# RetNet into a mixture of experts on one core: first half of expert 0's w2 asked for before two stores, and its first block difference made before the last logits

## Chip, cores and metric

The kernel runs on one core of a Trainium2 chip. The metric is device time in microseconds (us), here the median of three runs of the kernel.

## Reference

The reference computes a RetNet recurrence over q, k, v of 4 batches, 8 heads, 768 tokens and head size 64, and feeds the 3072 rows of 512 features into a mixture of 8 experts, of which each row takes the one with the largest logit:

```
state = gamma * state + k[t]^T v[t]        # per batch and head
y[t]  = (q[t] @ state) / sqrt(64)
x = y as rows (3072, 512)
logits = x @ w_gate                        # (3072, 8)
e = argmax(logits),  gate = softmax(logits)[e]
out[row] = gate * (relu(x[row] @ w1[e]) @ w2[e])    # w1: 512x1024, w2: 1024x512
```

All inputs and the result are float32.

## The kernel before

The attention part runs in 12 steps (the loop over `s`, line 863). A step takes 128 tokens of two batches: masked scores, the state's part and the new state on TensorE (PE), masks on VectorE (DVE), copies out of PSUM on ScalarE (ACT), scaling of q and v on GpSimd (POOL). The rows x of a step are turned on DVE (`to_rows`, line 653) one step later, and `store` (line 659) writes them from SBUF to a DRAM tensor `x_d` by four transfers of 128 KB, issued by SyncE (SP). Later on POOL's indirect transfers (`gather`, line 175) fetch the rows of an expert from `x_d`. Logits are made for two steps at a time (`logits`, `logits_of`); `place` turns them into ranks and places of the rows per expert, in three rounds.

From line 825 on the order of the instructions on all five engines is that of the program text. Each engine works through its own list in order, and an instruction that waits holds up what stands behind it on its engine. SP's transfers share eight semaphores in turn, so each also waits for the landing of the eighth transfer before it.

Expert 0 has an early pass: its first 256 rows (`EARLY`), which the first two rounds have found, are computed while the last rows are still being placed. Its weights w1 are asked for in a quarter, a quarter and a half (lines 922 to 926), w2 in two halves of 1 MB (`weights2`, line 160, and `more_of_weights2`, line 165; the first half holds feature blocks 0 to 3). In the last step (`last`, s = 11) SP stores the rows of steps 9 and 10 and then asks for the first half of w2.

After the loop, lines 972 to 975 run `layer1` for eight feature blocks f. In the midst of each block's four matmuls `within_early(f)` (line 945) adds what belongs to the last rows: at f = 1 the transposes of the last logits, their sum over four parts on DVE (L685) with what `place` makes of it, the turn of the last rows, their store and the request for the second half of w2; at f = 3 to 5 ranks and counts, and at the end of f = 5 the list `src` of source rows and a gather of two tiles on POOL; at f = 7 the first operands of the second layer.

The second layer of these 256 rows, `pair` (line 382), is a 2x2 block product with seven block products instead of eight (Strassen-Winograd). It needs four sums of blocks of h (`halves_of_h`, line 290, written to `he`) and four differences of blocks of w2 (`halves_of_w`, line 300, written to `we`). Of these, `we[0]` = b12 - b11 needs the first half of w2 alone, `we[1]` = b22 - we[0] and `we[2]` = b22 - b12 need the second half too. `we[0..2]` and `he[0..2]` are made on DVE; `we[3]` = b21 - we[1] and then `he[3]` on POOL (lines 980, 981), behind four gathers (lines 962 and 979). `he[0]` and `he[1]` are made for three of the four blocks at f = 7 (line 967) and for the last one at line 976. In `pair` the PE products come in the order ya (from h and w2 as they are), yb (he[1], we[1]), yd (he[2], we[2]), yc, ya again, ye (we[3]), yf (he[3]). Between them DVE makes the gated sums `u` and the output parts (`part`, L396) and, as `spare`, 16 transposes of the expert's further rows into `xTa` (L237); with these and the last parts done, PE begins the first layer of the further rows of expert 0 (L265, at 147.9 us). Later experts are not touched by the change.

Of the kernel before, what the change touches and what calls it, by code (L numbers as in the profile page):

```python
# [53 lines left out]
def kernel(  # L54
# [105 lines left out]
    def weights2(pool, e, parts=1, now=None):  # L160
        w2t = pool.tile([P, 1, FT, DM], F32, tag="w2t", name="w2t")
        more_of_weights2(w2t, e, parts, range(parts) if now is None else now)
        return w2t

    def more_of_weights2(w2t, e, parts, now):
        for part in (ts(i, FT // parts) for i in now):
            nc.sync.dma_start(w2t[:, :, part, :], w2v[:, ds(e, 1), part, :])
# [4 lines left out]
    first = ctx.enter_context(tc.tile_pool(name="first", bufs=1))  # L172
# [127 lines left out]
    def halves_of_w(w2t, ws, which=range(4), by=nc.vector):  # L300

        ws = [w.rearrange("p (f d) -> p f d", f=FH) for w in ws]
        b11, b12, b21, b22 = (w2t[:, 0, ts(j, FH), ts(k, DH)] for j in range(2) for k in range(2))
        sums = (b12, b11), (b22, ws[0]), (b22, b12), (b21, ws[1])
        for i in which:
            by.tensor_tensor(out=ws[i], in0=sums[i][0], in1=sums[i][1], op=ALU.subtract)  # L306
        return ws
# [175 lines left out]
    with ExitStack() as actx:  # L483
# [33 lines left out]
        def scale_q(s, b, by=nc.gpsimd, parts=1):  # L517
            got = raw.pop(("q", s, b))
            qs = raw["qs", s, b] = att.tile([P, 2, H, D], F32, tag="qs", name="qs")
            for part in (ts(i, H // parts) for i in range(parts)):  # L520
                for e in range(2):
                    by.tensor_tensor(out=qs[:, e, part, :], in0=got[:, part, ts(e, D)], op=ALU.mult,  # L522
                                     in1=inner(dec[:, ts(2 * where[s][0] + e, H)][:, part], D))
# [8 lines left out]
        def ends(s):  # L532
            return 2 * where[s][0] + where[s][2] == NC - 1
# [11 lines left out]
        def fade():  # L545

            back = dec[:, ts(2 * NC - 1, H)].rearrange("p (a j) -> p j a", j=2)
            for j in range(2):
                fading.append(xT1[:, j, :].rearrange("p (a t) -> p a t", a=HP))
                nc.gpsimd.tensor_tensor(out=fading[j], in0=middle(causal[:, :], HP), in1=inner(back[:, j, :], P), op=ALU.mult)  # L550
# [18 lines left out]
        def turn_k(s, b):  # L569
            kT = att.tile([P, HP, P], F32, tag="kT", name="kT")  # L570
            tr = pairs_of("tr", 2, "trk")
            heads_first(raw["k", s, b], tr)
            nc.scalar.copy(out=kT, in_=tr)  # L573
            front[s, b] = kT
# [4 lines left out]
        def scores(s, b):  # L579
            kT, qT = front.pop((s, b)), q_of(s, b)  # L580
            sc = [pairs_of("sc", 4, "sc") for _ in range(2)]
            am = [att.tile([P, HP, P], F32, tag=f"am{j}", name=f"am{j}") for j in range(2)]
            for a in range(HP):
                for j, half in ((0, 0), (1, 1), (1, 0), (0, 1)):
                    r, keys = ts(j, D), ts(half, P // 2)
                    nc.tensor.matmul(sc[j][keys, a, :], lhsT=kT[r, a, keys], rhs=qT[r, a, :], start=True, stop=True)  # L586

            def mask():
                for j in range(2):
                    nc.vector.tensor_tensor(out=am[j], in0=sc[j], op=ALU.mult,  # L590
                                            in1=fading[j] if ends(s) else middle(causal[:, :], HP))

            return am, mask
# [3 lines left out]
        def outputs():  # L597
            return [ps("y", 2, "y").rearrange("p (b a t) -> p b a t", b=2, a=HB) for _ in range(2)]
# [60 lines left out]
        def store(s):  # L659
            m, b1, e = where[s]  # L660
            xg = x.pop(("g", s))
            for g in range(Q):
                nc.sync.dma_start(x_d[ts((2 * m + e) * 2 + b1, 2 * P), ts(g, P)].rearrange("(t l) r -> l t r", l=L),
                                  xg[ts(g, L), :, :, :].rearrange("p b q r -> p (b q) r"))
# [145 lines left out]
        def load_all(nm, s):  # L810
            for b in range(2):
                load(nm, s, b)
# [46 lines left out]
        def step(s, at):  # L859
            for _ in range(WHEN.get(s, "").count(at)):  # L860
                next(rest, None)

        for s in range(STEPS):
            last = s + 1 == STEPS
            if s + 2 < STEPS:
                if s % 2 and s + 3 < STEPS:
                    load_all("q", s + 3)
                load_all("v", s + 2)
                if s + 3 < STEPS:
                    load_all("k", s + 3)  # L870
            if s % 2 == 0 and s + 2 < STEPS:
                for b in range(2):
                    scale_q(s + 2, b)
            if s + 1 < STEPS:
                (as_it_is if ends(s + 1) else scale_both)(s + 1)
            if s in (1, 2):
                nc.gpsimd.memset(xs2[s % 2], 0.0)
            if s == 3:
                fade()
            if s:  # L880
                am = [scores(s, b) for b in range(2)]
                am[0][1]()
                am[1][1]()
                step(s, "n")
            if last:
                pad_ranks(acc[:, NR - 1, 0:2])
            y = outputs()
            steps = [s - 2, s - 1] if s and s % 2 == 0 else []
            if where[s][0] or where[s][2]:
                with_state(s, y)  # L890

            def ahead():
                for b in range(2):
                    turn_k(s + 1, b)

            def ahead_q():
                if s % 2:
                    for b in range(2):
                        turn_q(s + 1, b)

            if s:
                if steps:
                    logit = logits(steps)
                if last:
                    early_rows()
                else:
                    ahead()
                reduce = logits_of(*logit) if steps else lambda: None
                step(s, "p")
                if not last:  # L910
                    ahead_q()
                reduce()
                if s in NEXT:
                    rest = chain(rest, place(NEXT.index(s) - 1))
                step(s, "a")
                to_rows(s - 1)
                if 2 <= s <= PART:
                    store(s - 2)
                if s == PART:
                    store(s - 1)  # L920
                if s == PART + 1:
                    wa = [weights1(first, 0, 4, [0])]
                if s == PART + 2:
                    more_of_weights1(wa[0], 0, 4, [1])
                    store(s - 2)
                    more_of_weights1(wa[0], 0, 2, [1])
                if last:
                    store(s - 2)
                    store(s - 1)
                    wa.append(weights2(first, 0, 2, [0]))  # L930
            next_state(s)()
            step(s, "b")
            within(s, y, am, ahead if s == 0 else lambda: step(s, "w"))
            step(s, "c")
            if s == PART + 2:
                fetched()
# [4 lines left out]
        we = [att.tile([P, FH * DH], F32, tag=tag, name="we", bufs=bufs)  # L941
              for tag, bufs in [("q", 4)] * 4]


        def within_early(f):
            nonlocal ne, arm, src, far, which
            if f == 1:
                logits_of(*logit)()
                next(rest)
                to_rows(STEPS - 1)  # L950
                store(STEPS - 1)
                more_of_weights2(wa[1], 0, 2, [1])
            if f == 3:
                next(rest)
            if f == 4:
                ne = count()
                arm = arms(ne)
            if f == 5:
                next(rest)
                next(rest, None)  # L960
                src, far = sources(inv, "")
                gather(xs2[0], src, range(HALF, TC))
            if f == 6:
                which = regs(0)
            if f == 7:
                halves_of_w(wa[1], we, [0])
                halves_of_h(hTa, hs, [0, 1], blocks=slice(0, FH - 1))
                halves_of_w(wa[1], we, [1])

# [287 lines left out]
```

## Time and profile before

| | |
|---|---|
| runs | 447.82, 444.72, 446.83 us; median 446.83 us |
| the profiled execution | 447.64 us, of which the span of the trace is 445.9 us |
| busy PE / weight loads / DVE / ACT / POOL | 425.8 / 373.4 / 243.0 / 125.3 / 270.2 us |
| chain that ended last | PE 64% of the span |
| mean granted clock of PE | 0.985 |

Times in the rows are microseconds from the start of the span. Engines: PE matmuls, PEld the weight loads of PE, DVE, ACT, POOL, and SPq the issuing of transfers on SP. L306 is line 306 of the kernel.

### The profile page before, as it was taken

To read this page: it belongs to the slowest core of one execution; us is meant where nothing else is said; L and a number is where in the kernel's file an instruction comes from. 1 tells how busy PE (TensorE), PEld (TensorE's weight loads), DVE (VectorE), ACT (ScalarE), POOL (GpSimd) and SP (SyncE) were. 2 spreads that over 40 slices of the span, in tenths; PEclk is the share of its full clock that TensorE was granted. 3 is DMA by queue.
4 is the path that set the end of the run, shared out by engine and by line. 5 is a ranking of instruction groups with operands and counts; after the bars stand their busy time and mean duration, and the time that the engine had idled before them with its cause. 6 is when DMAs were issued, how large, how long until landed. Compare 5 with 4: busy or idle time off the path is not lost.

```text
span 445.9 us, 10584 instructions
## 1 busy us (share of the span) xinstructions
PE 425.8 (95%) x4027; PEld 373.4 (84%) x4027; DVE 243.0 (54%) x541; ACT 125.3 (28%) x284; POOL 270.2 (61%) x223
## 2 busy tenths in 40 slices
PE   7899898989999899999999999999999999999992
PEld 4789787878788868879998999997999999699681
DVE  4544879496689946713562464356256335533320
ACT  2456353454411212310321321034022114112310
POOL 4469526442037358594819883899996698579111
PEclk9999999899999899999999999999999999999997
DMA  9999999999953699366232972496395268120001
GB/s 198 235 232 204 232 219 212 247 222 282 271 163 93 209 398 359 99 230 193 111 81 60 309 254 65 106 374 189 103 355 172 50 170 335 32 91 0 5 30 51
DMA packets 113326, 80.72 MB, mean 181 GB/s; under 512 B 56874, under 2 KB 97834, under 8 KB 113200
## 3 DMA queue, kind: packets, MB, share of 16 engines
q1 hardware_dynamic: 104336, 65.31, 52.7%
q0 software_dynamic: 5520, 12.60, 8.4%
q10 hardware_dynamic: 3344, 1.36, 1.3%
q8 instruction: 52, 0.85, 0.8%
q14 instruction: 74, 0.61, 0.4%
HBM read 60.88 MB, written 15.99 MB: 172 GB/s over the span
## 4 chain that ended last, share of the span: by engine, by line
PE 64%; DVE 0%; ACT 0%; issue 0%; POOLq 0%
PE p L344 25%; PE p L390 19%; PE p L278 8%; PE p L265 7%; PE p L1021 6%; DVE xs L396 0%; POOLq L1253 0%; ACT o L283 0%; ACT o L284 0%; DVE u L396 0%; DVE gate L228 0%; DVE o L396 0%
## 5 line engine op out<-in xcount | busy, mean ns | idle before, releaser
L177 POOL DMA_INDIRECT xs<-x_d,src x30 | 32.0, 1067 | 19.7 <-issue 7.2
L348 DVE TENSOR_TENSOR hT<-p,q 128x196 f32<-128x196 f32 (+5 forms) x72 | 25.9, 360 | 31.4 <-PE p L344 31.2
L437 POOL DMA_INDIRECT out_dram<-o,dst x20 | 20.0, 998 | 34.9 <-ACT o L286 13.8
L522 POOL TENSOR_TENSOR qs<-q,dec 128x512 f32<-128x512 f32 x22 | 23.3, 1088 | 29.0 <-DMA q<-in_q_dram 18.0
L278 PE MATMUL p<-w2t,hT 128*24 128x128 f32 (+6 forms) x288 | 37.6, 357 | 0.0
L390 PE MATMUL p<-ws,hs 128*128 128x256 f32 x168 | 37.4, 379 | 0.0
L344 PE MATMUL p<-t,w1t 128*128 128x196 f32 (+5 forms) x192 | 35.8, 329 | 0.0
L344 PE MATMUL p<-t,s 128*128 128x196 f32 (+5 forms) x192 | 35.8, 329 | 0.0
L396 DVE SCALAR_TENSOR_TENSOR q<-p,gate,q 128x256 f32<-128x256 f32 x28 | 12.8, 479 | 41.8 <-PE p L390 26.3
L390 PEld LDWEIGHTS p<-ws,hs 128*128 128x128 f32 x168 | 31.9, 190 | 4.3
L590 DVE TENSOR_TENSOR am<-sc,causal 128x512 f32<-128x512 f32 x40 | 24.9, 683 | 16.1 <-PE sc L586 16.1
L306 POOL TENSOR_TENSOR ws<-w2t,ws 128x1024 f32<-128x1024 f32 x14 | 33.1, 2363 | 0.5
L306 POOL TENSOR_TENSOR ws<-w2t 128x1024 f32<-128x1024 f32 x14 | 33.2, 2369 | 0.1
L344 PEld LDWEIGHTS p<-t,s 128*128 128x128 f32 x192 | 32.4, 190 | 0.0
L344 PEld LDWEIGHTS p<-t,w1t 128*128 128x128 f32 x192 | 32.4, 190 | 0.0
L278 PEld LDWEIGHTS p<-w2t,hT 128*24 128x24 f32 (+6 forms) x288 | 18.6, 123 | 16.1 <-issue 14.7
L348 DVE TENSOR_TENSOR q<-p,q 128x196 f32<-128x196 f32 (+5 forms) x48 | 17.1, 358 | 24.2 <-PE p L344 15.7
L396 DVE SCALAR_TENSOR_TENSOR o<-p,gate,q 128x256 f32<-128x256 f32 x21 | 10.2, 484 | 34.4 <-PE p L390 29.6
L390 PE MATMUL p<-w2t,hT 128*128 128x256 f32 x112 | 26.9, 381 | 0.1
L586 PE MATMUL sc<-qT,kT 64*64 64x128 f32 x768 | 24.8, 273 | 1.6 <-ACT kT L573 1.4
L528 POOL TENSOR_TENSOR vs<-v,dec 128x512 f32<-128x512 f32 x19 | 19.7, 1045 | 10.2 <-DMA v<-in_v_dram 9.6
L1021 PE MATMUL p<-hT,w2t 128*128 128x136 f32 (+2 forms) x192 | 25.7, 295 | 0.0
(221 smaller groups left out, 899.1 us busy)
## 6 DMA issues: line engine op xcount, KB each, us to landing
w1t<-in_moe_w_dram SPq DMA_DIRECT2D x7, 2048.0 KB, 11.3
w2t<-in_moe_w_dram SPq DMA_DIRECT2D x7, 2048.0 KB
k<-in_k_dram SPq DMA_DIRECT2D x24, 256.0 KB, 4.6
v<-in_v_dram SPq DMA_DIRECT2D x24, 256.0 KB, 5.2
x_d<-xg SPq DMA_DIRECT2D x48, 128.0 KB, 3.0
q<-in_q_dram SPq DMA_DIRECT2D x11, 512.0 KB
xs<-xs SPq DMA_DIRECT2D x80, 64.0 KB, 2.1
w2t<-in_moe_w_dram SPq DMA_DIRECT2D x2, 1024.0 KB
```

The lines of the kernel that those rows point to most:

```text
L177: nc.gpsimd.indirect_dma_start(out=xs[:, t, :], out_offset=None, in_=x_d[0:rows, :], in_offset=bass.IndirectOffsetOnAxis(ap=idx[:, t : t + ...
L265: nc.tensor.matmul(hp, lhsT=w1t[:, 0, dt, ts(f, P)], rhs=xT[:, dt, n0:n], start=(dt == 0), stop=(dt == DT - 1))
L278: nc.tensor.matmul(y[j * z : j * z + m, 0:c], lhsT=hT[:, f, t * P + r0 : t * P + r0 + m], rhs=w2t[:, 0, f, ts(j, c)], start=(i == 0), stop ...
L306: by.tensor_tensor(out=ws[i], in0=sums[i][0], in1=sums[i][1], op=ALU.subtract)
L344: nc.tensor.matmul(rows(y), lhsT=a(d, f), rhs=b(d), start=start and d == 0, stop=d == 1, skip_group_check=True)
L348: nc.vector.tensor_tensor(out=to, in0=rows(y), in1=rows(plus), op=ALU.add)
L390: nc.tensor.matmul(y, lhsT=a[:, f, :], rhs=b[:, f, :], start=start and f == 0, stop=f == FH - 1, skip_group_check=True)
L396: nc.vector.scalar_tensor_tensor(out=to, in0=y, scalar=g[i], in1=plus, op0=ALU.mult, op1=ALU.add)
L522: by.tensor_tensor(out=qs[:, e, part, :], in0=got[:, part, ts(e, D)], op=ALU.mult, in1=inner(dec[:, ts(2 * where[s][0] + e, H)][:, part], D))
L586: nc.tensor.matmul(sc[j][keys, a, :], lhsT=kT[r, a, keys], rhs=qT[r, a, :], start=True, stop=True)
L590: nc.vector.tensor_tensor(out=am[j], in0=sc[j], op=ALU.mult, in1=fading[j] if ends(s) else middle(causal[:, :], HP))
L1021: nc.tensor.matmul(y, lhsT=w2t[:, 0, f, ts(dt, P)], rhs=hT[:, f, EARLY : EARLY + m], start=(i == 0), stop=(i == FT - 1))
```

## The change

In the last step the request for the first half of w2 is put ahead of the two stores on SP. On DVE the difference `we[0]` is taken from f = 7 to f = 0 of `within_early`, ahead of the sum of the last logits. Nothing else is touched.

```
                 if last:
+                    wa.append(weights2(first, 0, 2, [0]))
                     store(s - 2)
                     store(s - 1)
-                    wa.append(weights2(first, 0, 2, [0]))
...
         def within_early(f):
             nonlocal ne, arm, src, far, which
+            if f == 0:
+                halves_of_w(wa[1], we, [0])
             if f == 1:
                 logits_of(*logit)()
                 next(rest)
...
             if f == 7:
-                halves_of_w(wa[1], we, [0])
                 halves_of_h(hTa, hs, [0, 1], blocks=slice(0, FH - 1))
                 halves_of_w(wa[1], we, [1])
```

On SP, around the last steps of the attention part (`x_d<-xg` are the stores, four to a step; `128x4x512` is a half of w1 or of w2):

```order
 L663 DMA x_d<-xg 32x8x128 x4
 L158 DMA w1t<-in_moe_w_dram 128x4x512
-L663 DMA x_d<-xg 32x8x128 x8
 L167 DMA w2t<-in_moe_w_dram 128x4x512
-L663 DMA x_d<-xg 32x8x128 x4
+L663 DMA x_d<-xg 32x8x128 x12
 L167 DMA w2t<-in_moe_w_dram 128x4x512
 L158 DMA w1t<-in_moe_w_dram 128x4x1024
```

The first half of w2 stands right behind the second half of w1; the eight stores of steps 9 and 10 stand behind it, and the four of step 11 follow these directly.

On DVE, where the places of the early rows end (`dst_e`) and the sum of the last logits (L685) begins:

```order
 L206 SCALAR_TENSOR_TENSOR far_e<-ct_e,far_e 128x2
 L207 SCALAR_TENSOR_TENSOR dst_e<-bt_e,far_e 128x2
+L306 TENSOR_TENSOR we<-w2t 128x1024
 L685 TENSOR_REDUCE lg<-lg 128x32
 L702 TENSOR_REDUCE mx<-lg 128x8
```

The difference `we[0]` now stands ahead of the sum L685, and everything behind that sum stands behind it too.

On DVE, where the source rows of the last round are known (`src`) and the operands of the second layer begin (`he`):

```order
 L191 SCALAR_TENSOR_TENSOR src<-tok,far 128x32
 L192 TENSOR_TENSOR far<-inv,far 128x32
-L306 TENSOR_TENSOR we<-w2t 128x1024
 L297 TENSOR_TENSOR he<-hTa 128x384
 L297 TENSOR_TENSOR he<-he,hTa 128x384
```

Here `he[0]` follows the list of source rows directly; the lists of PE, ACT and POOL have the same order as before.

## Rows read from the trace of the kernel before

**Rows 1.** Busy time by windows: stretch; PE, PEld, DVE, ACT, POOL busy (instructions); clock; DMA

```profile
116.00:138.00 22.00, 22.00 (x133) 17.73 (x130) 16.56 (x59) 6.24 (x15) 7.05 (x10) 1.00 0.60 170
```

**Rows 2.** Timeline of SP's issues, 102 to 128 us: start, length, engine, line, tiles, count

```profile
107.70 0.63 SPq L158 DMA_DIRECT2D w1t<-in_moe_w_dram  x1
109.06 9.13 SPq L663 DMA_DIRECT2D x_d<-xg  x8
118.24 0.48 SPq L167 DMA_DIRECT2D w2t<-in_moe_w_dram  x1
```

**Rows 3.** DMA packets of two stretches, 111 to 114.5 us, then 120 to 124 us

```profile
DMA packets 1037, 1.34 MB, mean 382 GB/s; under 512 B 57, under 2 KB 538, under 8 KB 1036
...
DMA packets 508, 1.01 MB, mean 252 GB/s; under 512 B 16, under 2 KB 16, under 8 KB 508
```

**Rows 4.** Timeline, DVE around the last logits and a weight load of PE

```profile
117.33 0.16 DVE L207 SCALAR_TENSOR_TENSOR dst_e<-bt_e,far_e 128x2 uint32<-128x2 int32 x1
...
121.10 0.29 DVE L685 TENSOR_REDUCE lg<-lg 128x32 f32<-128x128 f32 x1 [3.60 <-PE lg L684]
...
128.22 1.23 PEld L781 LDWEIGHTS <-here 128*128 128x128 bf16 x8 [0.23 <-DVE here L762]
```

**Rows 5.** Timeline of POOL, 129 to 150 us

```profile
131.03 2.00 POOL L177 DMA_INDIRECT xs<-x_d,src  x1 [6.17 <-DVE far L192]
133.34 1.39 POOL L177 DMA_INDIRECT xs<-x_d,src  x1 [0.30 <-issue]
135.03 1.03 POOL L177 DMA_INDIRECT xs<-x_d,src  x1 [0.30 <-issue]
136.37 1.16 POOL L177 DMA_INDIRECT xs<-x_d,src  x1 [0.31 <-issue]
137.55 2.36 POOL L306 TENSOR_TENSOR we<-w2t,we 128x1024 f32<-128x1024 f32 x1
```

**Rows 6.** Timeline of DVE, 130.2 to 149 us

```profile
130.90 1.22 DVE L306 TENSOR_TENSOR we<-w2t 128x1024 f32<-128x1024 f32 x1
132.69 0.56 DVE L297 TENSOR_TENSOR he<-hTa 128x384 f32<-128x384 f32 x1 [0.57 <-ACT hTa L267]
133.28 0.56 DVE L297 TENSOR_TENSOR he<-he,hTa 128x384 f32<-128x384 f32 x1
...
135.43 1.22 DVE L306 TENSOR_TENSOR we<-w2t 128x1024 f32<-128x1024 f32 x1
136.56 0.68 DVE L297 TENSOR_TENSOR he<-hTa 128x512 f32<-128x512 f32 x1
137.54 0.88 DVE L396 SCALAR_TENSOR_TENSOR u<-yp,gate_e,m 128x256 f32<-128x256 f32 x2 [0.30 <-PE yp L390]
```

**Rows 7.** Timeline of PE and its weight loads: product yd and those behind it; further rows

```profile
137.30 3.32 PEld L390 LDWEIGHTS yp<-we,he 128*128 128x128 f32 x16 [0.28 <-DVE he L297]
...
147.93 9.00 PE L265 MATMUL p<-xTa,w1t 128*128 128x112 f32 x64 [1.73 <-DVE gate L228]
```

**Rows 8.** Timeline, 48.8 to 52.1 us: DVE beside POOL's products of q

```profile
48.84 0.22 DVE L703 TENSOR_TENSOR dl<-lg,mx 128x64 f32<-128x64 f32 x1
48.93 4.05 POOL L522 TENSOR_TENSOR qs<-q,dec 128x512 f32<-128x512 f32 x4 [4.66 <-PE new L623]
...
50.06 0.99 DVE L706 TENSOR_TENSOR top<-top,em 128x64 f32<-128x64 f32 x1
```

**Rows 9.** Timelines of DVE and of POOL, 303 to 307 us

```profile
304.22 0.69 DVE L297 TENSOR_TENSOR hs<-hT 128x512 f32<-128x512 f32 x1
304.82 1.10 DVE L297 TENSOR_TENSOR hs<-hT,hs 128x512 f32<-128x512 f32 x1
...
302.25 4.01 POOL L1036 TENSOR_SCALAR of<-ofr,gate 128x512 f32<-128x512 f32 x2
```

**Rows 10.** Busy time by windows, columns as in the first group, behind the pair

```profile
138.00:148.00 10.00, 8.27 (x39) 6.97 (x38) 9.64 (x25) 0.47 (x1) 5.18 (x4) 1.00 0.20 57
...
149.00:153.00 4.00, 4.00 (x24) 4.00 (x23) 3.93 (x6) 0.91 (x4) 3.64 (x7) 0.57 0.92 285
```

More of the change, by code (lines that the diff above doesn't have):

```diff
@@ L927 @@
                 if last:
+                    wa.append(weights2(first, 0, 2, [0]))
                     store(s - 2)
                     store(s - 1)
-                    wa.append(weights2(first, 0, 2, [0]))
             next_state(s)()
@@ L946, in within_early @@
             nonlocal ne, arm, src, far, which
+            if f == 0:
+                halves_of_w(wa[1], we, [0])
             if f == 1:
@@ L965, in within_early @@
             if f == 7:
-                halves_of_w(wa[1], we, [0])
                 halves_of_h(hTa, hs, [0, 1], blocks=slice(0, FH - 1))
```

## Prediction

> **What bounds the kernel now.** I read the windows first: from 116 to 138 us PE is busy in all of 22.00 us [rows 1], so in this stretch nothing ends sooner unless PE's own list gets shorter or a wait between its weight loads goes. From 138 to 148 us PE has 8.27 of 10 us and DVE 9.64 [rows 10]: there DVE is the bound, and the idle time of PE stands in one piece, the 1.73 us ahead of the first layer of the further rows, put down to DVE [rows 7]. So the path is PE until its product yb is there, which releases DVE's first `u` at 137.54 after 0.30 us of waiting, and from then on DVE: sums, sixteen transposes, parts, and at 147.93 PE again [rows 6, 7]. The reader should see that both moved pieces lie ahead of 137.54, where DVE isn't the bound as a whole but has two places without slack: the chain from the last logits to `here`, for which PE waits 0.23 us [rows 4], and `he[2]`, for which PE waits 0.28 us [rows 7].
>
> **The request on SP.** It moves from 118.24, behind eight stores, to right behind the second half of w1, whose issue ends at 107.70 + 0.63 = 108.33 [rows 2]. It has as many bytes as before. It is queued behind w1's half: between 111 and 114.5 us 1037 - 538 = 499 packets of 2 KB or more went through, about the 512 that such a half has, at 382 GB/s [rows 3]. From 114.5 on 1.05 MB take 2.75 us at that pace, and 4.2 us at the 252 GB/s of the stretch in which this transfer ran before [rows 3]: landed at 117.3 to 118.7. The stores of steps 9 and 10 go behind it; their rows are fetched by a gather at 131.03 [rows 5], so some 3 us of delay are covered by about 10. One store of step 10 has to wait for w2's landing, since it is the eighth transfer behind it; what is queued behind that store is the store of step 11, whose rows are turned on DVE only after the sum at 121.10. Cost 0. Without the queue's order, w2 would share the rate with the gather of the early rows; that is a rival below.
>
> **The difference ahead of the logits.** we[0] costs 1.22 us [rows 6]. DVE ends `dst_e` at 117.49 and then waits 3.60 us for PE's logits until 121.10 [rows 4]. With w2 landed at 117.3 to 118.7 it ends at 118.7 to 119.9, at least 1.2 us ahead of the sum. Cost 0, cover 1.2 us; if that cover goes, each us more delays the sum, the ranks and `here`, and so PE.
>
> **The difference gone from f = 7.** DVE is free at 130.98 and not 132.12. But `he[0]` waits for the last relu but one of ACT, and did so for 0.57 us with we[0] in front of it [rows 6]. So it starts at 132.69 as before, and so does all behind it to `he[2]`. Gain 0; the upper bound is the 0.28 us that PE waits for `he[2]` [rows 7], and no row gives a reason for it.
>
> **What POOL does with it.** Here the change has an effect that its two lines don't show. The first gather began at 131.03 beside we[0] and took 2.00 us, where one with little beside it takes 1.03 [rows 5, 6]: it ended 0.91 us after we[0] had. Without we[0] I let it take 1.03: it ends at 132.06, and with 0.30 us between gathers the second runs from 132.36 to 133.39, before `he[1]` (133.28 to 133.84) matters. The third begins at 133.69, is held by `he[1]`, and by the measure of the second one before (133.84 + 0.89 = 134.73) ends at 134.73. The fourth begins at 135.03, exactly where the third did before, and ends as that did at 136.06 [rows 5]. So POOL is through its four gathers 1.47 us sooner, and begins its own difference we[3] at 136.08 instead of 137.55.
>
> At that moment DVE is in we[2] (135.43 to 136.65) and `he[2]` follows [rows 6]. All three read two operands from SBUF. What happens then is seen in the attention part: a product of two SBUF operands on DVE, dispatched at 50.06 beside the row of four of POOL, each some 1.01 us long, took 0.99 us, while an operation of the same shape took 0.22 [rows 8]; it ended with the POOL instruction of that time. So I let POOL wait for the end of we[2], take its turn at 136.65 and keep it: 2.36 us, less the 0.12 that a held start saved the first gather (0.91 against 1.03): 136.65 + 2.24 = 138.89. `he[2]` then ends 0.68 - 0.14 us later (the held product above ended 0.08 us behind POOL where 0.22 is its length), at 139.4 instead of 137.24.
>
> The Trainium skill (SBUF — State Buffer, section Who interferes with whom) says that a DVE instruction with two SBUF inputs and a GpSimd one that reads SBUF exclude each other for a whole instruction, and that the order of issue decides: by it POOL goes first and `he[2]` loses 2.2 us. The trace doesn't agree everywhere: by the one row against it the sum would lose 0.4 us [rows 9].
>
> **The sum.** PE has yd 2.2 us later, DVE makes `u` from 139.4 on instead of 137.54: +1.87 us, and from there DVE runs as before, one thing behind another, up to the parts. That alone sets the further rows to +1.9 us. PE's clock comes on top. After the idle 1.73 us before, the granted clock was 0.57 on the mean of 149 to 153 us, partly at 1.2 GHz, which is 4 x 0.43 = 1.7 us of work lost [rows 7, 10]. The new gap ahead of yd is longer (about 2.2 us), so I let the fall happen behind that one: PE would end the pair not at 148.4 (139.55 and the 8.85 us of five products) but at 150.1, the last part on DVE follows at 150.55, and the further rows begin at 150.7, +2.8. But then PE has idled there 0.6 us and not 1.73, and the fall behind it goes: -1.7. Net +1.1 us. The edits themselves are bounded by -0.28 and, for a later w2, by the rival below; the clock by -1.7 and +0.9 against the 1.9.
>
> The profiled execution would go from 447.64 (span 445.9) to 448.7; it lies 0.8 above the median of the runs, 446.83, from which I forecast 447.9 us. A measurement of this kernel tells about 1% (4.5 us) from no change, so this is no difference that such a bound shows.
>
> **Rivals.**
>
> *POOL's early start harms nothing (446.8 us).* For it: in a later expert POOL ran from 302.25 to 306.26 beside four differences of DVE, of which one was 0.4 us longer and the others weren't [rows 9]; DVE dispatches `he[2]` 0.09 us before we[2] ends [rows 6], so it may keep its turn. Or the fourth gather starts late enough to be held by we[2] again, as it was before. Against it: rows 8, and that the gathers of before did get their turn between two DVE operations. The Trainium skill (SBUF — State Buffer, the same section) says that a tensor_tensor, unlike a copy, doesn't stall the making of descriptors, and calls the reason inferred: by that POOL would not come forward at all and the time would be 446.8. The trace doesn't agree, with 2.00 against 1.03 us [rows 5].
>
> *w2 lands after the logits (slower).* Place: we[0] in front of L685. If it lands at t, the sum waits until t + 1.22, so from t = 119.9 on every us costs PE one, as it already waits 0.23 us for `here` [rows 4]. At the landing of before, about 123.6 (its packets fill 120 to 124 us [rows 3]), it would cost 3.7 us: 450.5; over 1% only from t = 124.4. Against it: it is asked for 10 us sooner, and only w1's half is in front.
>
> *w2 takes the rate from the early gather.* If the queues shared and did not keep order, the copies of the early rows would come up to 2.7 us (1 MB at 382 GB/s) later, and PE with them: 449.5. Against it: w1's half held the queue then, with and without w2.
>
> *The idle time is spread so that the clock doesn't fall (faster).* With `he[2]` late by under 0.5 us and the gap of 1.73 us cut, the 1.7 us come back: 445.1.
>
> **How the numbers follow.** Forecast 0.55 (its own range 446.9, no fall of the clock at all, to 449.7, a fall behind both gaps), no harm 0.29, w2 late 0.06, early gather 0.05, clock kept 0.05. The range 445.4 to 449.9 takes the first two with the spread of the runs and leaves out most of the late ones. Faster by over 1% is 0.02: no row offers 4.5 us. Slower by over 1% 0.04: a late w2 with the conflict on top. Within 1%: 0.94.
>
> **What would show it.** Right: SP's request for w2 at about 108.4; we[0] on DVE at 117.5 to 118.7, ending well ahead of L685 at 121.1; the first gather of `src` near 1.0 us; POOL's we[3] beginning at about 136.1; `he[2]` some 2.8 us long instead of 0.68; a wait of PE's weight load for it of over 2 us instead of 0.28; the further rows at 149.8 to 150.7. Wrong: we[3] at 137.5 again, or `he[2]` of 0.7 us beside it (then no harm); a DVE wait for a DMA ahead of L685 (then w2 is late); PE or ACT waiting longer for the gather of the early rows (then the rate is shared).

## The result, and the profile after

| | before | after |
|---|---|---|
| median of six runs | 447.06 us (444.72 to 449.63) | 452.75 us (451.70 to 453.93) |
| ratio, 95% interval | | 1.0135 (1.0098 to 1.0171) |
| the profiled execution | 447.64 us, span 445.9 | 452.32 us, span 450.1 |

The change makes the kernel slower, by 4.4 to 7.6 us with its interval. The forecast was 447.9 us, at most 449.9. Where the time went is seen where the prediction looked. The same stretches as [rows 1, 10], in the kernel after, with the third one shifted to where its first layer of the further rows now stands (stretch; PE, PEld, DVE, ACT, POOL busy; clock; DMA):

```profile
116.00:138.00 22.00, 21.44 (x134) 17.20 (x131) 15.83 (x56) 6.39 (x15) 5.83 (x10) 1.00 0.63 183
138.00:148.00 10.00, 6.01 (x20) 4.66 (x20) 9.12 (x13) 0.00 (x0) 5.73 (x4) 0.83 0.18 53
148.00:154.00 6.00, 5.46 (x27) 4.52 (x26) 5.58 (x15) 0.47 (x1) 0.00 (x0) 1.00 0.02 5
```

PE has 6.01 us in the ten from 138 on, where it had 8.27. DVE is still at 9.12, but with 13 instructions instead of 25: it is busy and gets little done. The granted clock of that stretch fell from 1.00 to 0.83. The timelines of SP, of DVE up to `he[2]`, and of POOL, kernel after (start, length, engine, line, tiles, count, idle time before and what ended it):

```profile
109.70 0.47 SPq L158 DMA_DIRECT2D w1t<-in_moe_w_dram  x1
110.21 1.05 SPq L167 DMA_DIRECT2D w2t<-in_moe_w_dram  x1
111.36 16.63 SPq L663 DMA_DIRECT2D x_d<-xg  x12
...
121.34 1.22 DVE L306 TENSOR_TENSOR we<-w2t 128x1024 f32<-128x1024 f32 x1 [3.53 <-DMA w2t<-in_moe_w_dram]
122.48 0.28 DVE L685 TENSOR_REDUCE lg<-lg 128x32 f32<-128x128 f32 x1
...
136.65 5.33 DVE L306 TENSOR_TENSOR we<-w2t 128x1024 f32<-128x1024 f32 x1
141.90 0.68 DVE L297 TENSOR_TENSOR he<-hTa 128x512 f32<-128x512 f32 x1
...
132.25 1.04 POOL L177 DMA_INDIRECT xs<-x_d,src  x1 [6.01 <-DVE far L192]
...
136.25 1.03 POOL L177 DMA_INDIRECT xs<-x_d,src  x1 [0.30 <-issue]
137.32 2.36 POOL L306 TENSOR_TENSOR we<-w2t,we 128x1024 f32<-128x1024 f32 x1
139.62 1.26 POOL L297 TENSOR_TENSOR he<-hTa,he 128x512 f32<-128x512 f32 x1
141.04 1.83 POOL L177 DMA_INDIRECT xs<-x_d,src  x1 [0.16 <-issue]
```

Three things stand here. The four gathers ahead of POOL's differences take 1.01 to 1.04 us each (the first and the last of them are shown), where the first took 2.00 and the second 1.39 [rows 5]. DVE's we[2] takes 5.33 us, where it took 1.22 [rows 6], and it ends (141.98) 1.10 us after the end of POOL's second difference (139.62 + 1.26 = 140.88): 1.22 us is its own length, so nearly all of it was done after POOL had finished both. And we[0] waited 3.53 us for w2, so the sum of the logits begins right behind it and not, as in [rows 4], when PE has the logits. PE, two rows of the kernel before, then the kernel after (the last row is cut off by the end of the window):

```profile
128.23 1.37 PE L781 MATMUL found<-val,here 128*128 128x160 bf16 x8
135.53 5.49 PE L390 MATMUL yp<-we,he 128*128 128x256 f32 x24
...
129.45 1.38 PE L781 MATMUL found<-val,here 128*128 128x160 bf16 x8 [0.53 <-DVE here L762]
...
142.63 5.41 PE L390 MATMUL yp<-we,he 128*128 128x256 f32 x16 [3.99 <-DVE he L297]
...
151.33 1.89 PE L390 MATMUL yp<-w2t,he 128*128 128x256 f32 x8
153.76 7.37 PE L265 MATMUL p<-xTa,w1t 128*128 128x112 f32 x64 [0.54 <-DVE xs L396]
160.97 4.46 PE L278 MATMUL p<-w2t,hT 128*112 128x512 f32 x10
```

The whole difference of the two spans can be read from PE's starts: from the second layer of the further rows (L278, which begins at 156.76 us before and at 160.97 after) to the end both profiles take 289.1 us. `found` begins at 128.23 before and at 129.45 after: +1.22, of which 0.32 was there already at the sum of the logits before the last (107.52 and 107.84) and 0.9 is the late w2. Then the new wait: +3.99. The sixteen matmuls behind it, partly at 1.2 GHz (10 x 0.17 = 1.7 us of work lost by the mean of 138 to 148), take 5.41 us instead of 3.6 (before, twenty-four of them took 5.49 without a gap, and eight take 1.89): +1.81. The gap ahead of the further rows is 0.54 instead of 1.73: -1.19. Their first layer, now at the full clock, is 7.37 long instead of 9.00 [rows 7]: -1.63. The sum is +4.20 us, and the spans differ by 450.1 - 445.9 = 4.2.

### The profile page after: what moved, and what is told of

Read it like the earlier page. It is cut to its first block, busy times and chain, and to the rows that moved or that the text cites. A ratio compares the mean times of both kernels' runs of the same rounds, so it can differ in the third digit from the quotient of the medians.

```text
span 450.1 us, 10585 instructions
## 1 busy us (share of the span) xinstructions
PE 426.6 (95%) x4027; PEld 373.7 (83%) x4027; DVE 248.0 (55%) x541; ACT 125.1 (28%) x284; POOL 269.9 (60%) x223
## 3 DMA queue, kind: packets, MB, share of 16 engines
q10 hardware_dynamic: 3344, 1.36, 1.3%
## 4 chain that ended last, share of the span: by engine, by line
PE 78%; DVE 8%; DMA 5%; SPq 5%; issue 2%; POOL 0%; ACT 0%; POOLq 0%; DVEq 0%
PE p L344 25%; PE p L390 19%; PE p L278 8%; PE p L265 6%; PE p L1022 6%; PE sc L586 3%; DMA w2t<-in_moe_w_dram 2%; PE yp L390 2%; SPq L514 2%; PE y L645 2%; DVE here L762 2%; PE trq L554 2%; DMA v<-in_v_dram 1%; PE trk L554 1%; PE new L623 1%
## 5 line engine op out<-in xcount | busy, mean ns | idle before, releaser
L278 PE MATMUL p<-w2t,hT 128*24 128x128 f32 (+6 forms) x288 | 37.6, 357 | 0.0
L278 PEld LDWEIGHTS p<-w2t,hT 128*24 128x24 f32 (+6 forms) x288 | 18.6, 123 | 16.1 <-issue 14.7
```

The lines of the kernel that those rows point to most:

```text
L278: nc.tensor.matmul(y[j * z : j * z + m, 0:c], lhsT=hT[:, f, t * P + r0 : t * P + r0 + m], rhs=w2t[:, 0, f, ts(j, c)], start=(i == 0), stop ...
```

## The experiments

Theory A: the loss is the hold. POOL, no longer held up by we[0], comes with its two differences at the moment in which DVE needs its own, and DVE waits for both. Theory B: the loss is the late w2 ahead of the logits, or the early rows' gather that shares the rate with it. The expectations call A the lock theory and B the late-w2 or transfer theory. Each ratio is to the kernel before in runs on the same chip.

**e1: the request alone.**

```diff
                 if last:
+                    wa.append(weights2(first, 0, 2, [0]))
                     store(s - 2)
                     store(s - 1)
-                    wa.append(weights2(first, 0, 2, [0]))
```

> Only the request for w2 is moved, we[0] stays at f = 7. Lock theory (POOL's we[3] and he[3] take the second SBUF read of DVE while we[2] and he[2] are due, about 4 us of the loss; the late w2 about 0.9 us): no loss, 446.5 to 447.6 us, the first gather again near 2.0 us, we[2] 1.2 us long. Transfer theory (what is lost is lost by the stores and gathers that stand behind w2): slower than before by 3 us or more, with a longer wait for the early gather or for the gather of src.

Measured: 447.13 against 446.79 us, ratio 1.0022 (0.9983 to 1.0060): no difference that this can show. In what matters DVE and POOL read as before, with the first gather at 2.00 us beside we[0] and we[2] at 1.22 us:

```profile
138.58 1.22 DVE L306 TENSOR_TENSOR we<-w2t 128x1024 f32<-128x1024 f32 x1
...
134.11 2.00 POOL L177 DMA_INDIRECT xs<-x_d,src  x1 [6.17 <-DVE far L192]
...
115.12 1.92 PE L852 MATMUL tre<-ident,xe 128*128 128x128 f32 x8 [2.91 <-ACT xe L844]
```

The last row looks like the rival of the shared rate: PE waits 2.91 us for the early rows. Run e9 decides about it.

**e2: the difference ahead of the logits alone**, with w2 asked for as late as before.

```diff
+            if f == 0:
+                halves_of_w(wa[1], we, [0])
             if f == 1:
...
             if f == 7:
-                halves_of_w(wa[1], we, [0])
```

> Only we[0] is moved ahead of the last logits, w2 is asked for behind the stores as before. Lock theory: we[0] waits for w2 until about 123.7, the logits' sum comes 3.7 us later, PE loses some 3.5 us there and the lock comes on top: 453.5 to 456.5 us. Late-w2 theory (the wait for w2 alone makes the loss and the long we[2] follows from it in some other way): the loss grows in proportion to the wait, 3.7 against 1.4 us, to 460 us or more.

Measured: 456.25 us, ratio 1.0221 (1.0140 to 1.0302). That is inside the range that the lock theory gave and below the 460 us of its rival. Both prices stand in one trace, that of the late w2 and that of the hold:

```profile
123.53 1.23 DVE L306 TENSOR_TENSOR we<-w2t 128x1024 f32<-128x1024 f32 x1 [6.39 <-DMA w2t<-in_moe_w_dram]
...
138.84 5.32 DVE L306 TENSOR_TENSOR we<-w2t 128x1024 f32<-128x1024 f32 x1
...
126.53 0.19 PE L729 MATMUL rk<-ohs,before 128*128 128x64 bf16 x1 [2.37 <-DVE ohs L709]
...
144.82 5.37 PE L390 MATMUL yp<-we,he 128*128 128x256 f32 x16 [3.98 <-DVE he L297]
```

The moved difference costs more without the request on SP, and the hold comes with the difference, here with w2 as late as 123.53 us.

**e3: the changed kernel, POOL's differences behind `he[2]`.** A copy of one column on POOL makes it wait; both edits stay.

```diff
         gather(xs2[1], src[:, ts(1, TC)], range(HALF))
+        nc.gpsimd.tensor_copy(rt([P, 1], "tick"), hs[2][:, 0:1])
         T = halves_of_w(wa[1], we, [3], nc.gpsimd)
```

> The changed kernel, and on POOL one copy of a column of he[2] ahead of we[3], so that POOL's two differences begin when DVE is through with he[2]. Lock theory: we[2] is 1.2 us and he[2] 0.7 us long again, PE waits under 0.5 us ahead of yd, and what is left is the late w2: 447.5 to 448.5 us. Late-w2 or transfer theory: the copy changes nothing, 452 to 453 us.

Measured: 446.72 us, ratio 0.9979 (0.9935 to 1.0023). The loss is gone, with both edits in place, and so is the price of a late w2 that was still expected: in this profile the sum of the logits waited 3.65 us for PE, not for w2. DVE, POOL and PE of this run:

```profile
138.97 1.22 DVE L306 TENSOR_TENSOR we<-w2t 128x1024 f32<-128x1024 f32 x1
...
138.57 1.04 POOL L177 DMA_INDIRECT xs<-x_d,src  x1 [0.30 <-issue]
140.85 0.19 POOL L981 COPY tick<-he 128x1 f32<-128x1 f32 x1 [1.24 <-DVE he L297]
141.01 2.34 POOL L306 TENSOR_TENSOR we<-w2t,we 128x1024 f32<-128x1024 f32 x1
...
139.07 5.49 PE L390 MATMUL yp<-we,he 128*128 128x256 f32 x24
...
150.70 7.37 PE L265 MATMUL p<-xTa,w1t 128*128 128x112 f32 x64 [0.95 <-DVE u L396]
```

PE runs its twenty-four matmuls without a gap again. The gather at 138.57 runs beside we[2] and neither is longer: here we[2] was dispatched into a gather that had begun, while the gather of [rows 5] met a difference that had begun.

**e4: the kernel before, POOL's differences ahead of its third and fourth gather**, so that they come early without either edit.

```diff
-        gather(xs2[1], src[:, ts(1, TC)], range(HALF))
         T = halves_of_w(wa[1], we, [3], nc.gpsimd)
         S = halves_of_h(hTa, hs, [3], nc.gpsimd)
+        gather(xs2[1], src[:, ts(1, TC)], range(HALF))
```

> The kernel before, with the two first gathers of expert 1's rows moved on POOL from ahead of we[3] and he[3] to behind them, so that POOL comes to we[3] at about 134.8 with neither of the two edits of the change made. Lock theory: a DVE operation with two SBUF operands between 134.9 and 137.2 is held for 2 to 4 us and PE waits ahead of yb or yd: 449 to 451.5 us. Late-w2 or transfer theory: no change, 446.5 to 447.6 us.

Measured: 452.08 us, ratio 1.0146 (1.0047 to 1.0246), a loss like that of the change, and 0.6 us above the expected range. The profiled execution was the shortest of its four (449.21 us) and shows less of it:

```profile
135.20 2.35 DVE L297 TENSOR_TENSOR he<-he,hTa 128x128 f32<-128x128 f32 x1
137.47 1.21 DVE L306 TENSOR_TENSOR we<-w2t 128x1024 f32<-128x1024 f32 x1
138.61 1.75 DVE L297 TENSOR_TENSOR he<-hTa 128x512 f32<-128x512 f32 x1
...
135.05 2.35 POOL L306 TENSOR_TENSOR we<-w2t,we 128x1024 f32<-128x1024 f32 x1 [0.34 <-DVE we L306]
137.69 2.11 POOL L297 TENSOR_TENSOR he<-hTa,he 128x512 f32<-128x512 f32 x1 [0.29 <-DVE he L297]
...
140.41 5.41 PE L390 MATMUL yp<-we,he 128*128 128x256 f32 x16 [2.11 <-DVE he L297]
```

Here the two engines take turns: `he[1]`'s last block (0.29 us alone) ends 0.15 us behind POOL's we[3], then DVE's we[2] passes while POOL's he[3] (1.26 alone) is held, then `he[2]` (0.68 alone) is. That is the picture the prediction had for the change.

**e5: the changed kernel again**, for a second profile of it.

> The changed kernel itself, beside the others on one chip. Lock theory: we[2] is held for about 4 us again (5.3 us long, POOL's we[3] and he[3] inside it), the further rows begin some 5.5 us later against L685 than before: 451.5 to 454 us. A theory of chance (the long we[2] is an accident of one execution) has we[2] at 1.2 us in this profile.

Measured: 454.37 us, ratio 1.0145 (1.0021 to 1.0269). we[2] takes 5.32 us (5.33 in the first profile) and PE waits 3.99 us as it did there, so the hold is no accident. The price of the late w2 is not the same each time: w2 is late here too, but the logits are later, as PE had itself waited 3.88 us for the early rows at 114 us, and the sum of the logits still had to wait for PE.

```profile
120.52 1.22 DVE L306 TENSOR_TENSOR we<-w2t 128x1024 f32<-128x1024 f32 x1 [2.51 <-DMA w2t<-in_moe_w_dram]
123.25 0.29 DVE L685 TENSOR_REDUCE lg<-lg 128x32 f32<-128x128 f32 x1 [1.51 <-PE lg L684]
```

**e6: the changed kernel, only POOL's second difference behind `he[2]`** (the copy of e3 one line further down, between T and S).

> The changed kernel with one copy of a column of he[2] on POOL between we[3] and he[3]: we[3] comes as early as in the changed kernel, he[3] only behind he[2]. If a POOL operation holds DVE until it ends, one at a time: we[2] ends when we[3] is through, some 1.3 us sooner than in the changed kernel (about 4 us long), and the time is 449.5 to 452 us. If DVE loses only to two POOL operations in a row: we[2] 1.2 to 2 us long and 446.5 to 448 us. If it is not POOL's operations at all: we[2] 5.3 us, 452 to 454 us.

Measured: 451.99 us, ratio 1.0128 (1.0048 to 1.0208).

```profile
136.80 4.11 DVE L306 TENSOR_TENSOR we<-w2t 128x1024 f32<-128x1024 f32 x1
...
137.47 2.35 POOL L306 TENSOR_TENSOR we<-w2t,we 128x1024 f32<-128x1024 f32 x1
141.58 0.19 POOL L982 COPY tick<-he 128x1 f32<-128x1 f32 x1 [1.76 <-DVE he L297]
...
141.57 5.41 PE L390 MATMUL yp<-we,he 128*128 128x256 f32 x16 [2.77 <-DVE he L297]
```

With one operation of POOL instead of two, we[2] is 1.22 us shorter and PE waits 1.22 us less: the second operation (1.26 us) cost nearly its whole length on the path. we[2] again ends 1.09 us behind POOL's (140.91 and 139.82).

**e7: the kernel before with POOL's scaling of q later.** The same hold stands in the attention part of both kernels [rows 8]. A copy on POOL puts the scaling of steps 4, 6 and 8 behind DVE's chain of that step (`ohs`, or `here` in step 6):

```diff
+        def behind(what, s):
+            nc.gpsimd.tensor_copy(rt([P, 1], f"tick{s}", BF16), what)
+            for b in range(2):
+                scale_q(s + 2, b)
...
-            if s % 2 == 0 and s + 2 < STEPS:
+            if s % 2 == 0 and s + 2 < STEPS and s not in (4, 6, 8):
...
+                if s in (4, 8):
+                    behind(ohs[:, 2 * (s - 4), 0:1], s)
...
+            if s == 6:
+                behind(found_here[0], s)
```

> The kernel before, with POOL's scaling of q put behind DVE's chains in steps 4, 6 and 8 of the attention part (each gated by one copy of a column of what the chain makes), as DVE operations there are 0.7 to 1.0 us long beside POOL's instead of 0.2. Lock theory: the operations of L705, L706, L709 and L762 are short again, the idle time of PE ahead of the first ranks (1.05 us) and of found (1.67 us) mostly goes, and with it the fall of the clock at 77.6 us: 2 to 4 us faster than before, 442.5 to 445 us. Otherwise, or where PE waits for q instead: 446 to 449 us.

Measured: 444.61 against 447.55 us, ratio 0.9934 (0.9894 to 0.9974): it beats both kernels and lies in the range expected. DVE's three operations that the scaling had held in step 4 (L705, L706, L709) take 0.20 to 0.22 us (0.71 to 0.99 before). The fourth, L762 in step 6, was expected to be short as well and still takes 3.00 us (4.74 before). What PE sees, around step 6:

```profile
72.70 0.71 PE L782 MATMUL found<-val,here 128*128 128x160 bf16 x8
73.40 0.63 PE L554 MATMUL trq<-ident,qs 128*128 128x128 f32 x4
74.36 0.66 PE L554 MATMUL trq<-ident,qs 128*128 128x128 f32 x4 [0.33 <-POOL qs L522]
```

Before, `found` stood there at 76.11 behind a wait of 1.67 us; now it has none, and PE waits three times 0.33 to 0.34 us for the scaling instead. The granted clock of 76 to 80 us is 1.00, 0.70 before. Part is given back: at 98.77 PE waits 2.68 us for `val`, 1.60 before, and the clock of 100 to 104 us is 0.57, 1.00 before.

**e8: the kernel before, further rows on banks (2, 3, 0, 1)** instead of (2, 3, 4, 5), against the 1.73 us of [rows 7].

> The kernel before, with the first layer of expert 0's further rows on other PSUM banks (2, 3, 0, 1 and not 2, 3, 4, 5), so that it need not wait for the last two parts that DVE takes from banks 4 and 5. If the 1.73 us ahead of it are a wait for these banks: PE begins there at about 146.3 instead of 147.9, the fall of the clock behind it goes, 443.5 to 445.5 us. If it is a wait for DVE's list as a whole: no change, 446 to 448 us.

Measured: 448.31 us, ratio 1.0023 (1.0001 to 1.0045): no gain. The wait in its profile is 0.64 us, but in e1 and e7, with the old banks, it is 0.53 and 0.56 us. So the short wait needs no other banks.

**e9: the kernel before, unchanged**, for a second profile.

> The kernel before, unchanged, for a second profile of it. Theory: the wait of 1.73 us ahead of the first layer of the further rows, and the fall of the clock behind it, are of that one execution; here the wait is 0.5 to 0.7 us, the 64 matmuls of the first layer take about 7.4 us instead of 9.00, and the distance from the last logits' sum to the second layer of the further rows is about 33 us instead of 35.66. Rival: they belong to the kernel before; the wait is 1.7 us again and the distance 35 to 36 us. we[2] takes 1.22 us and he[2] 0.68 in either case.

Measured in its one run: 453.01 us, on a chip on which the kernel before has a median of 451.25 us. The wait ahead of the further rows is 1.36 us, between the two expectations, and the clock doesn't fall behind it:

```profile
149.43 7.37 PE L265 MATMUL p<-xTa,w1t 128*128 128x112 f32 x64 [1.36 <-DVE xs L396]
156.64 7.03 PE L278 MATMUL p<-w2t,hT 128*112 128x512 f32 x16
...
114.11 1.97 PE L852 MATMUL tre<-ident,xe 128*128 128x128 f32 x8 [2.27 <-ACT xe L844]
```

So the kernel before does not have the fall of [rows 7, 10] in every execution; none of the other six profiles without the hold has one in that place. The last row answers e1: PE waits 2.27 us for the early rows without any early request of w2.

**e10: e7's edit and e3's together** (both edits of the change, the copy that holds POOL back, the later scaling).

> The later scaling of q with both edits of the change and the copy that holds POOL's difference back until he[2] is there. Theory: the edits take nothing from the path and give nothing to it, so the ratio is that of the later scaling alone, about 0.993 (0.989 to 0.997). Rival: with POOL out of the way in the attention part, the earlier request or the difference ahead of the logits shows its own price (0.9 us for a late w2, 3 to 4 us for late early rows), and the ratio is 0.996 to 1.002.

Measured: 450.79 against 451.25 us on that chip, ratio 0.9978 (0.9938 to 1.0017): inside the rival's range (0.996 to 1.002) and just outside the theory's (0.989 to 0.997), with an interval that reaches into both, so neither is decided for. Nothing in its profile is late by the edits: we[0] at 119.72 waited 0.78 us for w2, the sum waited 1.59 us for PE, PE had the early rows without a wait, we[2] took 1.22 us. Nothing here shows a gain by the two edits even so: e7 without them has the lower ratio (0.9934), on another chip and with intervals that overlap.

## Why the prediction was wrong

**The chain was right up to POOL's we[3]; who goes first there, and the gain by the clock, were not.** POOL's gathers did come through sooner once we[0] was gone. Shifted by the 1.22 us that this profile is later at `found`, the forecast has POOL's starts within 0.02 us: 136.08 + 1.22 = 137.30 for we[3], and 137.32 was measured. we[3] did meet DVE's differences, PE did wait for `he[2]`, and the clock did fall behind the new gap and not behind the old one.

**The step that failed first: "I let POOL wait for the end of we[2], take its turn at 136.65 and keep it: 2.36 us".** It had one operation of POOL between we[2] and `he[2]`, gave POOL's he[3] right behind it no price, and came to a PE wait of some 2.2 us. The traces show POOL ahead of we[2] itself, with both its operations: 3.6 us of POOL, and a wait of 3.99 us (three profiles: 3.99, 3.99, 3.98). e6 isolates the second operation at 1.22 us. The further rows then began 4.6 us later than before (153.76 - 147.93, less the 1.22 at `found`) where the sum had 2.8; with this step alone put right, the forecast would have been about 449.7 us, an estimate, and still inside its range. The row that the step was built on [rows 8] shows a short product that waited for one operation of four, and e4 shows turns as well; neither says that DVE always gets its turn after one. The term should have kept both ends: one operation or all that POOL has in a row.

**The step that failed second: "PE has idled there 0.6 us and not 1.73, and the fall behind it goes: -1.7".** The gain was real in this pair of profiles (7.37 against 9.00), but the fall was no property of the kernel. The distance from the last sum of logits (L685) to the second layer of the further rows (L278), in every profile:

| profile | PE's wait for `he[2]`, us | L685 to L278, us |
|---|---|---|
| before [rows 4, 7] | none | 35.66 |
| e1, e3, e7, e8, e9, e10 | none | 32.92, 33.25, 32.87, 32.95, 33.67, 33.47 |
| e4 (turns) | 2.11 | 36.87 |
| e6 (one operation) | 2.77 | 37.68 |
| after, e5, e2 (two operations) | 3.99, 3.99, 3.98 | 38.49, 39.66, 38.47 |

Six of seven profiles without the hold lie near 33.2, and the one shown ahead of the prediction is the exception, by 2.5 us. Against 33.2 the hold costs 5.3 us in the profile after, and 6.2 with the 0.9 us of the late w2; the span difference is 4.2, and the 5.7 us between the medians lie nearer to the first sum. That the runs behind the median of before are mostly without that fall is an inference from these profiles, not a measurement of them.

**The request.** The landing was put at 117.3 to 118.7, with SP's issue at 108.4. DVE's waits for w2 ended at 121.34, 119.77, 120.52, 119.11 and 119.72 (after, e3, e5, e6, e10). SP's issue began at 108.6 to 110.2 in these, 110.21 in the profile after, as w1's half ahead of it went out at 109.70 and not at 107.70 [rows 2]; and from there it took 9.9 to 11.9 us where the prediction had 8.9 to 10.3. So the term was too short, by 0.4 to 2.6 us against its later end. The sum of the logits still waited for PE in four of five profiles (1.51 to 3.65 us); in e5 it did so only because the logits were later as well, and in the profile after the late w2 cost 0.9 us. The rival had the right place; the spread of SP's issue and of the landing can use up such a cover. The prediction gave 0.04 to a loss of over 1%, by a late w2 with the conflict on top. Both came, but the conflict was the larger part.

**The rivals.** No harm by POOL: refuted by e3 and e6. Late w2: a minor part once, and the whole of it only without the request (e2). Shared rate: with the early request PE's wait ahead of the early rows' transposes was none in the profiles after, e6 and e10, and 2.91, 3.62 and 3.88 in e1, e3 and e5; without it none in before, e2, e7 and e8, 1.06 in e4 and 2.27 in e9. Whether the request makes it likelier stays open; e1's and e3's times show no price for it, though e1's interval still allows 0.6%, some 2.7 us. Clock kept: refuted.

The Trainium skill (SBUF — State Buffer, section Who interferes with whom) has the order of issue decide, and the loser wait for a whole instruction. In e4 the trace agrees; in the profile after the loser waited for two, and took 5.33 us in all instead of 1.22. It also says that a tensor_tensor doesn't stall the making of descriptors. Here the gather at 141.04, begun while we[2] had its time, took 1.83 us instead of 1.03. But a gather also reads `src` from SBUF, and one that had begun first was not longer (1.04 us in e3), so no run shows which part of it was held.

## What to carry to other kernels

When an instruction is taken away from one engine, look at what the other engine was held by until then: the gain there moves its next work forward, and that may meet yours at the worst place. Price a conflict between DVE and POOL by the whole row of POOL's operations that can come, not by one, and try to fix it with a wait on POOL (one column copied, 0.19 us) where POOL has time: in e3 that gave back all of the loss. And take a fall of the clock from more than one execution before it is entered in a sum.

## What the runs showed of the hardware that was not expected

A held DVE instruction can lose more than one turn: 5.33, 5.32 and 5.32 us for 1.22 us of work against two operations of POOL back to back, 4.11 us against one, and it ended 1.09 to 1.10 us behind POOL's last each time. By the records it had begun 0.65 to 0.67 us before POOL's first, and why it hadn't the right of way then is open; the starts on POOL are rough. The gather ahead of POOL's first is not enough to explain it: it had begun 0.39 to 0.40 us before we[2] in these four profiles, and 0.40 us before it in e3 and e10, where POOL's next instruction had to wait and we[2] took 1.22 us. In e4, where POOL waited 0.29 us between its two, DVE passed in between; but the product of [rows 8] also passed between two that had no such pause. POOL's operations were not longer for it (2.36 and 1.26 us) when they won.

Executions differ by more than the effects sought here: PE's wait for the early rows is between 0 and 3.9 us, the wait ahead of the further rows between none (e4) and 1.73. From 60 to 124 us, the granted clock falls between 72 and 84 us in six of the twelve profiles, between 100 and 108 in four and between 112 and 124 in four. The kernel before has a median of 446.79 us on one chip, 447.55 on another and 451.25 on a third.
